# Second block's attention moved into slots 0 and 1, two tiles to a power, in a fused attention, feed-forward and soft-MoE kernel

## The chip, the cores and the metric

The kernel runs on one core of a Trainium2 chip. The metric is device time in microseconds (us), the median of several runs. The engines are TensorE (PE, with its weight loads PEld), VectorE (DVE), ScalarE (ACT), GpSimd (POOL) and SyncE (SP), which issues most of the DMAs.

## The reference

```python
def _attn_ref(q, k, v, g_norm):
    kv = np.einsum('bhsd,bhse->bhde', k, v)
    out = np.einsum('bhsd,bhde->bhse', q, kv)
    rms = np.sqrt(np.mean(out * out, axis=-1, keepdims=True) + 1e-06)
    return (out / rms * g_norm).astype(np.float32)

def _moe_ref(x, w_in, w_out):          # x: 4608 x 512, w_in: 512 x 2048, w_out: 2048 x 512
    h = x @ w_in
    g = h * np.cos(h)
    return (g @ w_out).astype(np.float32)
...
# then a soft mixture: 32 slots, softmax over tokens, 8 experts, softmax over slots
```

Attention is linear: for each head a 64x64 matrix `kv`, then `q @ kv`, divided by its root mean square over the 64 columns of the head. Its output, 4608 tokens by 512, feeds the feed-forward layer, and that feeds the mixture.

## The kernel before

The 4608 tokens are cut into ten blocks, eight of 512 tokens (blocks 0 to 7) and two of 256. A block has tiles of 128 tokens. For a block, each of 16 **slots** f (feature tiles of 128 of the 2048 hidden columns) does one `main(j, f)`: 12 products of 128x512 in fp32r, since each operand is split in a high and a low part and three of the four part products are taken, over four slices of the 512 input columns. `h` comes out in one of three PSUM banks (pool `ps_m`). Then `fr_tt` (ACT, whole turns), `round_off` (DVE, rest), `cos_b` (ACT, sine table), `cos_c` (DVE, `h` times the cosine, named gT or q) follow, and `cos_c` frees the bank.

A tile of attention goes through four steps. `att_out` does the products with `kv` on PE, a square on ACT, a sum by head on DVE (L213), a scale (L214) and, on POOL, the power -1/2 of 8 sums for each token (L216, result `ri`). `att_xs` multiplies by `ri` on DVE (L223). `att_xT` transposes on PE (L241) and scales into the high part on ACT (L245); `att_lo` takes the low part on DVE (L254). The small tiles `ss` (the sums) and `ri` come from a pool whose `bufs` says how many live at once: a tile that takes a buffer again waits for all readers of the one before.

The sixteen weight tiles of `w_in` are made in six steps `A R P L H S`: A scales on ACT (L301), R, P, L work on bits on DVE (L306, L311, L316), H takes the high part on ACT (L322), S the low part on POOL (L327). All of them go through two staging buffers `st_m`. Small letters are the same steps of `w_out`.

Order is written out by hand. `PLAN["start"]` lists the work before slot 0: the attention of block 0 (`ao`, `xs`, `xT`, `lo`), weight tiles 0 and 1, and `warm.n`, n products of 128x128 that only fill PE. `one` lists the steps of slots 0 to 3, where only block 0 has mains; `two` those of slots 4 on, where block 0 and block 1 run in turn with a lag of four slots, so block 1's `x` must be ready at slot 4 (`m0` is block 0's main of the slot, `m1` block 1's, `s` the extra work of the slot, `p` what comes after `r`, `c` the last step). `PLAN["A"]` gives the slots in which `att_out` and the steps behind it run for blocks 1 and 2, `PLAN["ao"]`, `xs`, `xT`, `lo` for later blocks, one block ahead of use. From block 2 on a slot has one main.

```python
        ss = sm_p.tile([128, H], F32, tag="ss", name="ss", bufs=4)
        nc.vector.tensor_reduce(out=ss, in_=sq, axis=AX.X, op=ALU.add)
...
        nc.gpsimd.tensor_tensor(out=ri[:, :, 0], in0=ss, in1=mhalf, op=ALU.pow)
```

Of the kernel before, what the change touches and what calls it, by code (L numbers as in the profile page):

```python
# [37 lines left out]
    ),  # L38
    one='m0 e0 A R f0 P a l0 r0 p0 L r s0 b0 H p c0 S l',
    two='s0 m0 A R m1 a f0 e1 P L l0 f1 r0 r1 s1 l1 p0 r b0 H c0 e0 b1 p c1 l S p1',  # L40
    wm=(3, 5),
# [31 lines left out]
def tile_linear_attention__ffn_cos__soft_moe(  # L73
# [309 lines left out]
    def main(j, f, ps=None):  # L383
        if ps is None:
            ps = ps_m.tile([128, 512], F32, tag="h", name="h")
        w, x = w_t[f], xt_t[j]
        assert all((j, t) in x_done for t in range(TT[j])) and ("S", f, 0) in done
        n = 0
        for kk in range(KD):
            for a, b in ((0, 0), (0, 1), (1, 0)):  # L390
                nc.tensor.matmul(out=ps, lhsT=w[:, a, kk, :], rhs=x[b][:, kk, :],  # L391
                                 start=(n == 0), stop=(n == 3 * KD - 1))
                n += 1
        h_t[j, f] = ps
# [583 lines left out]
    for b in range(1, B):  # L978
# [4 lines left out]
        for pr in range(4):  # L983
            at2(n, sl[pr], kv_pair, b, pr)

    for j in range(1, NB):
        n = min(j - 1, SMALL - 1)
# [101 lines left out]
    def token(t, f):  # L1089
        k, *arg = t.split(".")  # L1090
        if k.upper() in steps:
            out = int(k.islower())
            ws = [int(arg[0])] if arg else [w for w in range(NF) if PLAN["co"][w] == f] if out else [f + PLAN["LI"]]
            for w in ws:
                if w < NF and (arg or out or w >= PLAN["PI"]):
                    ck(k.upper(), w, out)
                    steps[k.upper()](w, out)
        elif arg:
            a = int(arg[0])
            dict(kv=lambda: kv_pair(0, a), ao=lambda: att_out(0, a), xs=lambda: att_xs(0, a),  # L1100
                 xT=lambda: att_xT(0, a), lo=lambda: att_lo(0, a), warm=lambda: warm(a),
                 win=lambda: load_win(a), wout=lambda: load_wout(a), lkv=lambda: load_kv(a // 4, a % 4),
                 rem=lambda: load_rem(a) if a == 0 else load_kz(0, 1),
                 q=lambda: [load_q(a, t) for t in range(3 if a else TT[0])])[k]()
        else:
# [6 lines left out]
    with tc.manual_schedule():  # L1112
# [132 lines left out]
```

## Time and profile before

| what | value |
|---|---|
| median of 3 runs | 675.74 us (674.06, 675.74, 676.40) |
| the profiled execution's own time | 674.39 us |
| its span, first to last instruction | 672.6 us |
| PE busy | 646.0 us, 96% of the span |
| DVE, ACT, POOL busy | 496.1, 328.1, 208.3 us |
| granted TensorE clock, mean | 0.991 of full speed |

The span is what the trace shows, and lies 1.8 us under the execution's own time. A busy time is a sum over the span. A row of the timeline gives start, length, engine, line, operation and count, and in brackets how long the engine had been idle and what ended that. PE records of f32 products are passes: a product of 128x128 in f32 has two, a transpose and an fp32r product one.

### The profile page before, as it was taken

The page shows a single profiled execution, that of the slowest core. Times are in us where ns is not written, and L with a number is a line of the kernel's source. Part 1 is how long each engine was busy: PE and PEld are TensorE (multiplying, and loading weights), DVE is VectorE, ACT ScalarE, POOL GpSimd, SP SyncE. Part 2 cuts the span into 40 slices and gives each one's busy share as a digit, 9 for nine tenths or more (in the row PEclk, how much of TensorE's full clock was granted, in tenths as well). Part 3 has the DMA queues.
Part 4 walks back from the last instruction along what each step waited for, and adds up shares of the span by engine and source line. Part 5 has one row for each costly group of instructions (what it writes and reads, how often), then busy time and mean ns, then how long its engine had stood idle before and what let it go on. Part 6 is the DMA issues. An engine that isn't in the chain of part 4 may idle for free.

```text
span 672.6 us, 12593 instructions
## 1 busy us (share of the span) xinstructions
PE 646.0 (96%) x4639; PEld 474.7 (71%) x4639; DVE 496.1 (74%) x909; ACT 328.1 (49%) x589; POOL 208.3 (31%) x291
## 2 busy tenths in 40 slices
PE   6989999999999999999999999999999999999992
PEld 6767777776667776767677677767677778984451
DVE  3799989966677778877887788787877765546143
ACT  3576767645244454445444554544463453552042
POOL 2451111320363333530643253334526322200000
PEclk9899999999999999999999999999999999999997
DMA  9955564111385636783677287576645369899998
GB/s 328 346 192 188 189 228 149 60 35 63 84 200 141 173 79 187 209 234 118 170 212 209 66 207 208 158 212 148 162 122 118 70 166 315 295 413 408 406 416 353
DMA packets 70589, 135.13 MB, mean 201 GB/s; under 512 B 10752, under 2 KB 39040, under 8 KB 69504
## 3 DMA queue, kind: packets, MB, share of 16 engines
q1 hardware_dynamic: 63360, 119.63, 54.3%
q0 software_dynamic: 7168, 14.69, 9.5%
q8 instruction: 37, 0.61, 0.4%
q14 instruction: 24, 0.20, 0.1%
HBM read 91.29 MB, written 13.63 MB: 156 GB/s over the span
## 4 chain that ended last, share of the span: by engine, by line
PE 76%; DVE 8%; ACT 5%; DMA 5%; SPq 2%; issue 2%; POOL 1%; DVEq 0%; ACTq 0%
PE h L391 46%; PE ab L624 5%; PE ops L202 4%; PE l L525 3%; PE xTps L241 2%; PE eh L780 2%; PE eo L817 2%; DMA g<-tr 2%; PE kvps L183 2%; PE tr L494 2%; DVE gT L453 2%; PE l L534 2%; DVE tmp L410 2%; ACT tmp L414 1%; SPq L513 1%
## 5 line engine op out<-in xcount | busy, mean ns | idle before, releaser
L391 PE MATMUL h<-xt,w 128*128 128x512 f32 (+1 forms) x1920 | 420.8, 374 | 3.6 <-DVE gT L453 1.5
L391 PEld LDWEIGHTS h<-xt,w 128*128 128x128 f32 x1920 | 329.4, 189 | 86.4 <-issue 12.7
L414 ACT ACTIVATE tmp<-tmp,hpi 128x512 f32<-128x512 f32 (+1 forms) x145 | 104.2, 720 | 174.2 <-DVE tmp L410 174.1
L513 POOL DMA_DIRECT2D g<-tr x224 | 123.4, 554 | 102.5 <-DVE tr L472 48.8
L453 DVE TENSOR_TENSOR gT<-tmp,h 128x512 f32<-128x512 f32 x130 | 89.1, 686 | 70.5 <-ACT tmp L414 70.5
L216 POOL TENSOR_TENSOR ri<-ss,mhalf 128x8 f32<-128x8 f32 x36 | 59.5, 1655 | 203.7 <-DVE ss L214 203.5
L410 DVE SCALAR_TENSOR_TENSOR tmp<-h,tmp 128x512 f32<-128x512 f32 (+1 forms) x145 | 97.1, 673 | 18.1 <-ACT tmp L407 17.2
L407 ACT ACTIVATE tmp<-h 128x512 int32<-128x512 f32 (+1 forms) x145 | 85.1, 587 | 46.7 <-PE h L391 46.4
L472 DVE STREAM_TRANSPOSE tr<-gT 128x512 f32<-128x512 f32 x103 | 73.2, 711 | 5.9 <-DMA g<-tr 1.6
L327 POOL TENSOR_TENSOR w<-st_m,w 128x512 fp32r<-128x512 f32 x16 | 21.4, 1335 | 63.8 <-ACT w L322 63.8
L202 PE MATMUL ops<-kvA,q 128*128 128x128 f32 (+1 forms) x320 | 38.6, 278 | 0.1
L245 ACT ACTIVATE xt<-xTps,gn 128x512 fp32r<-128x512 f32 x36 | 24.5, 685 | 25.7 <-PE xTps L241 25.7
L202 PEld LDWEIGHTS ops<-kvA,q 128*128 128x128 f32 (+1 forms) x320 | 34.6, 180 | 3.0 <-issue 2.0
L624 PE MATMUL ab<-g,d 128*32 128x512 f32 x256 | 32.3, 593 | 0.0
L525 PE MATMUL l<-gT,wp 128*32 128x512 f32 (+1 forms) x248 | 30.9, 556 | 0.0
L254 DVE SCALAR_TENSOR_TENSOR xt<-xTps,gn,xt 128x512 fp32r<-128x512 f32 x36 | 26.1, 729 | 4.8 <-ACT xt L245 4.6
L211 ACT ACTIVATE sq<-ops 128x512 f32<-128x512 f32 x31 | 18.5, 596 | 21.7 <-PE ops L202 21.6
L213 DVE TENSOR_REDUCE ss<-sq 128x8 f32<-128x512 f32 x31 | 21.0, 676 | 7.5 <-ACT sq L211 7.2
L183 PEld LDWEIGHTS kvps<-kv 128*64 128x64 f32 x448 | 15.4, 137 | 12.5 <-issue 7.6
L624 PEld LDWEIGHTS ab<-g,d 128*32 128x32 f32 x256 | 9.5, 110 | 19.2 <-issue 16.6
L223 DVE TENSOR_TENSOR sq<-ops,ri 128x512 f32<-128x512 f32 x31 | 20.9, 675 | 1.2 <-POOL ri L216 1.2
L241 PE MATMUL xTps<-ident,sq 128*128 128x128 f32 x124 | 19.0, 276 | 1.8 <-DVE sq L223 1.8
(186 smaller groups left out, 605.3 us busy)
## 6 DMA issues: line engine op xcount, KB each, us to landing
kv<-in_kv SPq DMA_DIRECT2D x28, 512.0 KB, 5.7
g<-tr SPq DMA_DIRECT2D x224, 64.0 KB, 3.7
g<-tr POOLq DMA_DIRECT2D x224, 64.0 KB, 3.8
ew<-in_ew SPq DMA_DIRECT2D x23, 512.0 KB, 8.9
q<-in_qT SPq DMA_DIRECT2D x36, 256.0 KB, 6.0
out<-ot SPq DMA_DIRECT2D x11, 768.0 KB, 7.5
rw<-in_w_in SPq DMA_DIRECT2D x16, 512.0 KB, 4.2
nat<-in_w_out SPq DMA_DIRECT2D x16, 512.0 KB, 3.9
```

The lines of the kernel that those rows point to most:

```text
L202: nc.tensor.matmul(out=ps[p0:p0 + n, pr * 128:(pr + 1) * 128], lhsT=q_t[j, t][:, pr, p0:p0 + n], rhs=kvbd[b % 2][:, pr, :], start=True, st ...
L216: nc.gpsimd.tensor_tensor(out=ri[:, :, 0], in0=ss, in1=mhalf, op=ALU.pow)
L241: nc.tensor.transpose(ps[:, kk * 128:(kk + 1) * 128], xs[:, kk * 128:(kk + 1) * 128], ident)
L391: nc.tensor.matmul(out=ps, lhsT=w[:, a, kk, :], rhs=x[b][:, kk, :], start=(n == 0), stop=(n == 3 * KD - 1))
L407: nc.scalar.activation(out=t.bitcast(I32), in_=ps, func=AF.Copy, bias=0.25, scale=INV_2PI)
L410: nc.vector.scalar_tensor_tensor(out=t, in0=ps, scalar=INV_2PI, in1=t.bitcast(I32), op0=ALU.mult, op1=ALU.subtract)
L414: nc.scalar.activation(out=t, in_=t, func=AF.Sin, bias=hpi, scale=TWO_PI)
L453: nc.vector.tensor_tensor(out=g, in0=fr, in1=h_t.pop((j, f)), op=ALU.mult)
L472: nc.vector.transpose(out=tr_t[j, q][:, :, i, :], in_=gT_t[j, n * q + i].rearrange("p (b t) -> p b t", t=32))
L513: (nc.gpsimd if b % 2 else nc.sync).dma_start(out=dst[32 * b:32 * b + 32, :, x, a:a + n, :].rearrange("p t f i -> p t (f i)"), in_=src[32 ...
L525: nc.tensor.matmul(out=l_t[j][32 * o:32 * o + 32, :], lhsT=wp[:, f, :], rhs=gT_t.pop((j, f)), start=(c == 0), stop=(c == (2 if j == NB - 1 ...
L624: nc.tensor.matmul(out=ps[32 * c:32 * c + 32, :], lhsT=d[:, t, :], rhs=gs[c // 2][t][:, (c % 2) * 512:(c % 2) * 512 + 512], start=(t == 0) ...
```

## The change

In the start list, `keep.7` adds seven filling products in a bank of `ps_m` between block 0's `att_out` and its first transpose; the last two `warm` lose one product; `xs.3` goes ahead of the first `lo`; scale A of weight tile 2 moves ahead of `lo.3`. The first main takes its products with the high part of `x` first. Slot 0 and slot 1 get lists of their own: `turn_on` in slot 0 does H and S of weight tile 2 and A, R, P of tile 3, so that S of tile 3 stands at slot 1's head. From slot 2 on, A is that of the tile one further on and stands before H. Block 1's `att_out` run in slots 0, 0, 1, 1, and its tiles share `ss2`, `ri2` in pairs, with one power of 128x16 for two tiles. The single `ss` and `ri`, which blocks 0 and 2 to 9 use, have two buffers, where there were four. The fourth `q` tile of block 1 is loaded with the other three, in a staging buffer. For blocks 3 on, the second `att_out` runs in slot 4, where it was in slot 5.

```diff
-        "kv.3 lkv.7 rem.1 q.1 win.3 wout.0 wout.1 wout.2 ao.0 ao.1 ao.2 ao.3 A.0 xs.0 xT.0 warm.4 xs.1 R.0 P.0 xT.1 "
-        "xs.2 L.0 H.0 S.0 xT.2 warm.3 lo.0 xs.3 lo.1 xT.3 lo.2 A.1 lo.3 R.1 P.1 L.1 H.1 S.1 "
+        "kv.3 lkv.7 rem.1 q.1 win.3 wout.0 wout.1 wout.2 ao.0 ao.1 ao.2 ao.3 keep.7 A.0 xs.0 xT.0 warm.4 xs.1 R.0 P.0 xT.1 "
+        "xs.2 L.0 H.0 S.0 xT.2 warm.2 xs.3 lo.0 lo.1 xT.3 lo.2 A.1 A.2 lo.3 R.1 P.1 L.1 H.1 S.1 "
...
-    one='m0 e0 A R f0 P a l0 r0 p0 L r s0 b0 H p c0 S l',
-    two='s0 m0 A R m1 a f0 e1 P L l0 f1 r0 r1 s1 l1 p0 r b0 H c0 e0 b1 p c1 l S p1',
+    one0='m0 e0 R f0 P l0 r0 p0 L s0 b0 c0',
+    one1='m0 e0 L f0 H S a l0 r0 p0 r s0 b0 A p c0 l',
+    one='m0 e0 R f0 P a l0 r0 p0 L r s0 b0 A H p c0 S l',
+    two='s0 m0 R m1 a f0 e1 P L l0 f1 r0 r1 s1 l1 p0 r b0 A H c0 e0 b1 p c1 l S p1',
...
-    A=(((0, 0, 1, 2), (1, 1, 1, 1), (2, 2, 3, 3), (0, 0, 0, 0)),
+    A=(((0, 0, 1, 1), (1, 1, 1, 1), (2, 2, 3, 3), (0, 0, 0, 0)),
...
-    ao=(2, 5, 8, 11),
+    ao=(2, 4, 8, 11),
...
-        ss = sm_p.tile([128, H], F32, tag="ss", name="ss", bufs=4)
+        pair = j == 1
+        if pair and t % 2:
+            s2, r2 = two.pop()
+        elif pair:
+            s2, r2 = (sm_p.tile([128, 2 * H], F32, tag=x, name=x, bufs=1) for x in ("ss2", "ri2"))
+            two.append((s2, r2))
+        if pair:
+            ss, ri = s2[:, t % 2 * H:t % 2 * H + H], r2[:, t % 2 * H:t % 2 * H + H].rearrange("p (h o) -> p h o", o=1)
+        else:
+            ss = sm_p.tile([128, H], F32, tag="ss", name="ss", bufs=2)
+            ri = sm_p.tile([128, H, 1], F32, tag="ri", name="ri", bufs=2)
...
-        ri = sm_p.tile([128, H, 1], F32, tag="ri", name="ri", bufs=4)
-        nc.gpsimd.tensor_tensor(out=ri[:, :, 0], in0=ss, in1=mhalf, op=ALU.pow)
+        if pair and t % 2:
+            nc.gpsimd.tensor_tensor(out=r2, in0=s2, in1=mhalf[:, 0:1].to_broadcast([128, 2 * H]), op=ALU.pow)
+        elif not pair:
+            nc.gpsimd.tensor_tensor(out=ri[:, :, 0], in0=ss, in1=mhalf, op=ALU.pow)
...
+        order = [(kk, a, b) for kk in range(KD) for a, b in ((0, 0), (0, 1), (1, 0))]
+        if (j, f) == (0, 0):
+            order.sort(key=lambda o: o[2])
...
+    def turn_on():
+        for k, w in (("H", 2), ("S", 2), ("A", 3), ("R", 3), ("P", 3)):
+            ck(k, w, 0)
+            steps[k](w, 0)
+
+    at(0, 0, turn_on)
```

Three places show how the instructions stand. The first is DVE in the start list, block 0's four tiles; `ss_...` are the sums, `st_x` the squares and later the scaled tiles, `ri_...` the powers, and the brackets name the semaphores of the engines that an instruction waits for. Before:

```order
L213 TENSOR_REDUCE ss_260<-st_x_126 128x8 [waits Activation_49]
L213 TENSOR_REDUCE ss_271<-st_x_126 128x8 [waits Activation_49]
...
L213 TENSOR_REDUCE ss_282<-st_x_126 128x8 [waits Activation_49]
L214 TENSOR_SCALAR ss_282<-ss_282 128x8 [waits DVE_49]
L223 TENSOR_TENSOR st_x_126<-ops_243,ri_252 128x512 [waits PE_49,Pool_49]
```

With the change:

```order
L228 TENSOR_REDUCE ss_261<-st_x_126 128x8 [waits Activation_49]
L228 TENSOR_REDUCE ss_272<-st_x_126 128x8 [waits Activation_49,Pool_49]
...
L228 TENSOR_REDUCE ss_283<-st_x_126 128x8 [waits Activation_49,Pool_49]
L229 TENSOR_SCALAR ss_283<-ss_283 128x8 [waits DVE_49]
L240 TENSOR_TENSOR st_x_126<-ops_244,ri_251 128x512 [waits PE_49]
```

The third and fourth sums now also wait for POOL, and the first multiplication by `ri` still stands behind the fourth sum.

The second is POOL from the start into slot 3: powers `ri`, and S of the weight tiles (`w`). Before:

```order
L216 TENSOR_TENSOR ri<-ss,mhalf 128x8 [waits DVE_49] x4
L327 TENSOR_TENSOR w<-st_m,w 128x512 [waits DMAHW4_49,Activation_49]
L327 TENSOR_TENSOR w<-st_m,w 128x512 [waits DMAHW5_49,Activation_49]
L216 TENSOR_TENSOR ri<-ss,mhalf 128x8 [waits DVE_49,Pool_49] x2
L327 TENSOR_TENSOR w<-st_m,w 128x512 [waits DMAHW0_49,Activation_49]
L216 TENSOR_TENSOR ri<-ss,mhalf 128x8 [waits DVE_49,Pool_49]
```

With the change:

```order
L233 TENSOR_TENSOR ri<-ss,mhalf 128x8 [waits DVE_49] x2
L233 TENSOR_TENSOR ri<-ss,mhalf 128x8 [waits DVE_49,Pool_49] x2
L344 TENSOR_TENSOR w<-st_m,w 128x512 [waits DMAHW4_49,Activation_49]
L344 TENSOR_TENSOR w<-st_m,w 128x512 [waits DMAHW5_49,Activation_49]
L344 TENSOR_TENSOR w<-st_m,w 128x512 [waits DMAHW0_49,Activation_49]
L231 TENSOR_TENSOR ri_443<-ss_442,mhalf 128x16 [waits DVE_49]
L344 TENSOR_TENSOR w<-st_m,w 128x512 [waits DMAHW0_49,Activation_49]
L231 TENSOR_TENSOR ri_495<-ss_494,mhalf 128x16 [waits DVE_49,Pool_49]
```

S of tile 2 now stands ahead of block 1's powers, and four powers of 128x8 became two of 128x16.

The third is PE in block 3, slots 3 to 6: `ldT` is a transpose of the block before's logits, `ops` the products of `att_out`, `xTps` those of `att_xT`. Before:

```order
L391 MATMUL h<-xt,w 128x512 x24
L594 MATMUL ldT<-ident,ld 128x64 x4
L391 MATMUL h<-xt,w 128x512 x12
L241 MATMUL xTps<-ident,sq 128x128 x4
L202 MATMUL ops<-kvA,q 128x128 x4
L391 MATMUL h<-xt,w 128x512 x12
```

With the change:

```order
L409 MATMUL h<-xt,w 128x512 x24
L611 MATMUL ldT<-ident,ld 128x64 x4
L207 MATMUL ops<-kvA,q 128x128 x4
L409 MATMUL h<-xt,w 128x512 x12
L258 MATMUL xTps<-ident,sq 128x128 x4
L409 MATMUL h<-xt,w 128x512 x12
```

The second `att_out` now stands between `ldT` and the main of slot 5. Blocks 4 to 7 are the same.

## Rows read from the trace of the kernel before

**Rows 1.** The page, busy us, share of the span and instructions of each engine

```profile
PE 646.0 (96%) x4639; PEld 474.7 (71%) x4639; DVE 496.1 (74%) x909; ACT 328.1 (49%) x589; POOL 208.3 (31%) x291
```

**Rows 2.** Waits of PE: who for whom, us in total, times, longest

```profile
PE xTps L241 <- DVE st_x L223: 2.3, 1, 2.3
...
PE xTps L241 <- DVE sq L223: 1.8, 1, 1.8
PE h L391 <- DVE gT L453: 1.5, 6, 0.3
...
PE h L391 <- POOL w L327: 1.0, 1, 1.0
```

**Rows 3.** Windows: stretch, length, busy us (instructions) of PE, PEld, DVE, ACT, POOL, PEclk, DMA

```profile
30.00:48.00 18.00, 15.22 (x101) 12.80 (x97) 16.43 (x32) 12.98 (x24) 10.23 (x7) 1.00 0.64 217
48.00:65.00 17.00, 16.74 (x98) 13.52 (x96) 16.53 (x29) 12.61 (x24) 4.07 (x3) 1.00 0.45 161
65.00:90.00 25.00, 25.00 (x174) 19.43 (x173) 24.67 (x41) 17.48 (x36) 3.93 (x3) 1.00 0.60 211
```

**Rows 4.** Timeline of the start, block 0's attention to the first main

```profile
13.75 6.57 POOL L216 TENSOR_TENSOR ri<-ss,mhalf 128x8 f32<-128x8 f32 x4 [11.54 <-DVE ss L214]
...
14.56 0.69 DVE L213 TENSOR_REDUCE ss<-st_x 128x8 f32<-128x512 f32 x1
...
16.17 0.17 DVE L214 TENSOR_SCALAR ss<-ss 128x8 f32<-128x8 f32 x1
16.26 1.50 DVE L223 TENSOR_TENSOR st_x<-ops,ri 128x512 f32<-128x512 f32 x2
...
20.60 0.68 DVE L223 TENSOR_TENSOR st_x<-ops,ri 128x512 f32<-128x512 f32 x1
...
22.23 0.60 PE L241 MATMUL xTps<-ident,st_x 128*128 128x128 f32 x4
22.87 0.69 ACT L245 ACTIVATE xt<-xTps,gn 128x512 fp32r<-128x512 f32 x1 [0.72 <-PE xTps L241]
...
23.61 0.50 PE L391 MATMUL h<-xt,w 128*128 128x512 f32 x1 [0.78 <-ACT xt L245]
...
24.40 2.83 PE L391 MATMUL h<-xt,w 128*128 128x512 f32 x11 [0.28 <-DVE xt L254]
```

**Rows 5.** Windows of 1 us in the start, columns as in the third group

```profile
19.00:20.00 1.00, 0.94 (x5) 0.78 (x5) 1.00 (x3) 0.00 (x0) 1.00 (x1) 0.50 1.01 406
```

**Rows 6.** Timeline of slots 0 to 5: idle DVE, PE's waits, H on ACT

```profile
27.45 1.05 DVE L306 TENSOR_SCALAR st_m<-st_m 128x512 int32<-128x512 int32 x1 [1.32 <-ACT st_m L301]
...
31.34 0.69 DVE L213 TENSOR_REDUCE ss<-sq 128x8 f32<-128x512 f32 x1 [0.92 <-ACT sq L211]
...
32.90 0.62 ACT L322 ACTIVATE w<-st_m 128x512 fp32r<-128x512 f32 x1
...
36.90 2.56 PE L391 MATMUL h<-xt,w 128*128 128x512 f32 x10 [1.03 <-POOL w L327]
...
47.16 0.63 PE L241 MATMUL xTps<-ident,sq 128*128 128x128 f32 x4 [1.75 <-DVE sq L223]
...
56.24 1.20 DVE L311 SCALAR_TENSOR_TENSOR st<-st 128x512 int32<-128x512 int32 x1
```

**Rows 7.** Groups on POOL by form: busy us, mean ns of one

```profile
L216 POOL TENSOR_TENSOR ri<-ss,mhalf 128x8 f32<-128x8 f32 x36 | 59.5, 1655 | 203.7 <-DVE ss L214 203.5
L327 POOL TENSOR_TENSOR w<-st_m,w 128x512 fp32r<-128x512 f32 x16 | 21.4, 1335 | 63.8 <-ACT w L322 63.8
...
L1229 POOL MEMSET const-float32-1.0<- 128x1 f32 x1 | 0.1, 98 | 0.0
```

**Rows 8.** Timeline of block 4, slots 4 to 6

```profile
310.05 0.69 DVE L453 TENSOR_TENSOR gT<-tmp,h 128x512 f32<-128x512 f32 x1 [1.32 <-ACT tmp L414]
310.08 0.46 PE L594 MATMUL ldT<-ident,ld 64*128 64x64 f32 x4
...
310.79 3.02 PE L391 MATMUL h<-xt,w 128*128 128x512 f32 x12 [0.25 <-DVE gT L453]
...
314.09 1.06 PE L202 MATMUL ops<-kvA,q 128*128 128x128 f32 x8
```

More of the change, by code (lines that the diff above doesn't have):

```diff
@@ L151, in load_q @@
             q_t[j, t] = first["q"][:, t]
+        elif (j, t) == (1, 3):
+            q_t[j, t] = first["wo"][3].rearrange("p (r c) -> p r c", r=4)
         else:
@@ L195, in tile_linear_attention__ffn_cos__soft_moe @@
     kv_done, x_done, g_done = set(), set(), set()
+    two = []
     def att_out(j, t):
@@ L204, in att_out @@
                                  start=True, stop=True)
-        if (j, t) == (1, 2):
-            sq = first["wo"][2].rearrange("p (h d) -> p h d", d=D)
+        if j == 1 and t > 1:
+            sq = first["wo"][4 - t].rearrange("p (h d) -> p h d", d=D)
         elif j:
@@ L387, in main @@
         assert all((j, t) in x_done for t in range(TT[j])) and ("S", f, 0) in done
[L388 to L393, printed above, removed]
+        order = [(kk, a, b) for kk in range(KD) for a, b in ((0, 0), (0, 1), (1, 0))]
+        if (j, f) == (0, 0):
+            order.sort(key=lambda o: o[2])
+        for n, (kk, a, b) in enumerate(order):
+            nc.tensor.matmul(out=ps, lhsT=w[:, a, kk, :], rhs=x[b][:, kk, :],
+                             start=(n == 0), stop=(n == 3 * KD - 1))
         h_t[j, f] = ps
@@ L744, in c_lo, with warm @@
         nc.vector.tensor_tensor(out=lo, in0=ps, in1=hi.bitcast(F32), op=ALU.subtract)
-    def warm(n):
-        ps = at_bank("warm")
+    def warm(n, ps=None):
+        if ps is None:
+            ps = at_bank("warm")
         for _ in range(n):
@@ L994, in tile_linear_attention__ffn_cos__soft_moe @@
             i = T0[j] + t + 3
-            if i < NT:
+            if 7 < i < NT:
                 jj = max(x for x in range(NB) if T0[x] <= i)
@@ L1092, in token @@
             out = int(k.islower())
-            ws = [int(arg[0])] if arg else [w for w in range(NF) if PLAN["co"][w] == f] if out else [f + PLAN["LI"]]
+            ws = [int(arg[0])] if arg else [w for w in range(NF) if PLAN["co"][w] == f] if out else [f + PLAN["LI"] + (k == "A")]
             for w in ws:
-                if w < NF and (arg or out or w >= PLAN["PI"]):
+                if w < NF:
                     ck(k.upper(), w, out)
@@ L1099, in token @@
             a = int(arg[0])
-            dict(kv=lambda: kv_pair(0, a), ao=lambda: att_out(0, a), xs=lambda: att_xs(0, a),
+            dict(kv=lambda: kv_pair(0, a), ao=lambda: att_out(0, a), xs=lambda: att_xs(0, a), keep=lambda: warm(a, ps_m.tile([128, 512], F32, tag="h", name="h")),
                  xT=lambda: att_xT(0, a), lo=lambda: att_lo(0, a), warm=lambda: warm(a),
@@ L1103, in token @@
                  rem=lambda: load_rem(a) if a == 0 else load_kz(0, 1),
-                 q=lambda: [load_q(a, t) for t in range(3 if a else TT[0])])[k]()
+                 q=lambda: [load_q(a, t) for t in range(4)])[k]()
         else:
@@ L1135, in tile_linear_attention__ffn_cos__soft_moe @@
         for f in range(NF):
-            for t in (PLAN["one"] if f < L else PLAN["two"]).split():
+            for t in PLAN[f"one{f}" if f < 2 else "one" if f < L else "two"].split():
                 token(t, f)
```

## The prediction

> **What bounds the kernel now.** I read the page first: PE is busy 646.0 of 672.6 us [rows 1], so only what PE idles can be won without less work, some 27 us. The waits of PE come next, since they say where that idleness lies and who ends it. Outside the first load and the tail they are few: 2.3 us before block 0's first transpose, which waits for the multiplication by `ri`; 1.8 once before a transpose of block 1; 1.0 once for a weight tile's low part on POOL; and six waits for gT of 0.3 at most [rows 2]. The windows then tell which engine paces the work behind those waits. From 30 to 48 us DVE is busy 16.43 of 18.00, from 48 to 65 it is busy 16.53 of 17.00 while PE is 16.74, and from 65 to 90 PE is full and DVE 24.67 of 25.00 [rows 3]. So from 30 to 90 us two engines are nearly full, and a lead that PE gets in slots 0 to 3 lasts only if DVE gets it too. That is the point on which the start's part of the sum turns. In blocks 3 to 7 the waits for gT are one in each block, 0.25 in block 4, in slot 5, because the cosine came late from ACT [rows 8].
>
> **The start list.** All times here are those of the trace. Block 0's four powers run one behind the other from 13.75, 6.57 us in all, 1.64 each, and the four sums ran ahead of them [rows 4]. With two buffers, the third sum must wait until the first power has read its buffer: 15.39, where it began at 14.56. The fourth waits for the second power: 17.04. Its scale begins 0.72 later (as 14.56 was followed by 15.28), and the first multiplication, which is queued behind it on DVE, at 17.9, where it was at 16.26. The third power needs the buffer of the first `ri`, so that multiplication must end first: 17.9 and 0.7 is 18.6. Third and fourth power end at 21.9, where they ended at 20.32. So the new wait stops the queue of DVE, and through it POOL's, PE's and ACT's.
>
> The fourth multiplication begins at 21.9, where it was 20.60; the list puts it ahead of the low part that it stood behind, so it is 1.3 late and not 1.6. It ends at 22.6. Two filling products (four passes at 1.06/8, which is 0.13 [rows 8], together 0.5) and the transpose follow, and ACT takes its step 0.64 after the transpose began (22.23 to 22.87), at 23.7, where it was 22.87. The first main begins 0.74 behind that, at 24.45, where it was 23.61: **0.83 late**. Its products with the low part come last now, so the hole between 23.61 and 24.40 goes: 12 products take 3.1 instead of 3.6, and it ends 0.3 late. DVE is 0.83 late with the low part, as ACT is.
>
> The seven filling products are fourteen passes at 0.13, 1.8 us, and lie in the hole of 2.3 before the first transpose. But that hole moves: PE now idles some 2 us behind them, until 18.6. The granted clock was 0.50 at 19 to 20 us, which is 1.2 GHz, after that idleness [rows 5]. I expect the same again. It costs nothing where PE waits for the powers anyway. If the first main still ran at 1.2 GHz, its 12 products would cost 12 x 0.24 more, 2.9, of which the hole of DVE in slot 0 (next part) takes 2.0: so 0 to 0.9, and I take 0, since the clock was full again before that main in the trace and PE's work ahead of it is of the same kind.
>
> **Slots 0 to 5.** PE loses both its waits there, 1.03 and 1.75 [rows 6]: S of tile 2 stands ahead of the powers, and block 1's last two tiles come a slot earlier. With 0.3 lost at the start, PE could reach slot 4 as much as 2.5 us early. DVE decides what is left of that. It starts 0.83 late. Its idleness of 1.32 before R of tile 2 goes, since A of that tile is earlier, and so does the 0.92 before block 1's first sum [rows 6]. But R of tile 3 now stands there and waits for A of tile 3, which on ACT stands behind the eight copies of `kv`, which end 0.3 late, and behind H of tile 2. The first sum could begin at 31.34 because a square of 0.6 had begun at 30.7, and ACT was free for it from 30.2. From 30.5, H takes 0.62 and A about as much, so R can begin at 31.75. DVE will have been free since 31.34 - 0.92 - 1.32 + 0.83, which is 29.9, or a little earlier: a new hole of 1.9 to 2.2. In all 0.83 - 2.24 + 2.0 is 0.6 late. Bit steps of DVE that fall on a POOL step are long (1.05 and, in 56.24's row, 1.20 [rows 6]); which ones do will change, worth 0.5 either way. Short holes in 30 to 65 (2.0 in all by rows 3, of which 0.92 is counted) may give back a few tenths. I take **0.5 late** at slot 5, bounds -0.3 and 1.2. PE's lead ends in waits for gT in slots 4 and 5.
>
> **The power of two tiles.** The trace has the power only at 128x8, 1.655 [rows 7]. At 128x16 it costs at least that, if the price is by instruction. At most it costs twice that less one start of an instruction, for which a memset of 128x1 at 0.098 stands: 3.21. I take 2.0, near the lower end: a subtraction costs 1.335 for 512 columns, 0.0026 a column, and with twenty such steps for a power (a guess, no row has it) eight more columns cost 0.4. Between the second scale and the multiplication that waits for the power stand three steps of DVE in the first pair (gT, L, rest; about 1.7 in all) and four in the second (2.2). So 2.0 costs 0.3 - 0 = **0.3**, 1.66 costs nothing, and 3.21 costs 1.5 + 1.0 = 2.5.
>
> Apart from these rows there is a rule: the Trainium skill's page "GPSIMD Engine Reference", section 3.1, has GpSimd spend a dispatch for each instruction and then cycles for each element, nothing else, so that a pair would save one dispatch alone. It has no price for a power; by it the sum would be that of the first rival. The subtraction's row fits it, and no row here shows a second width of the power.
>
> **Blocks 2 to 7.** In blocks 3 to 7, the second `att_out` fills the wait of slot 5. In block 4, gT ended at 310.74, `ldT` began at 310.08 and the main at 310.79. With eight passes between (1.06), the main starts behind gT and the wait is gone. The idle time was 0.25; the time lost was up to 0.4, since passes that follow each other overlap in the stream and `ldT`'s 0.46 holds its drain. Five times 0.35 is **-1.75**, bounds 0 and -2.1. The sum and scale that come earlier (0.69 and 0.17 [rows 4]) lie on a DVE that has holes there, 1.32 in that row alone. In block 2 they go ahead of the copy `d` for which the slot sums wait: 0 to 0.86, I take 0.2. A ahead of H in each slot delays H and the second cosine by 0.6 and frees ACT at the next slot's head; a weight tile has a slot of slack, so 0. The removed loads and the earlier `q` tile shift SP's queue by 256 KB in the start; tile 3, behind it, is needed over 10 us after its issue: 0.
>
> **Sum.** 0.5 + 0.3 + 0.2 - 1.75 = -0.75 against the profiled execution's own 674.39 (span 672.6 and 1.8 around it): 673.6. That execution lies 1.35 under the median of the runs, 675.74, so for a median I give **675.0**.
>
> **Rivals.** (1) The power is paid by column, 3.21. DVE stands 1.5 and 1.0 before the two pairs in place of 0.3: +2.2, so 1.45 over before, 677.2; with a first main at 1.2 GHz (+0.9) 678.1. This is the slower side, and it decides from a power of about 2.5, where the two waits (0.8 and 0.3) eat the rest of the gain. For it: the small price of starting an instruction [rows 7]. Against: eight columns would have to cost eighty times a subtraction's each. (2) DVE does catch up: its bit steps miss POOL's, and PE keeps 1.7 of its 2.5 at slot 4. Then -1.7 + 0.2 - 1.75 is -3.25, 672.5. For it: both of PE's large waits go. Against: 16.53 of 17.00 [rows 3]. (3) The wait in blocks 3 to 7 moves to the next main, as DVE has more to do before it: +1.0, 676.7. Against: the slot sums of slot 6 (16 products) give DVE time.
>
> **Chances.** Forecast 0.47, rivals 0.28, 0.13, 0.12. A measurement of this kernel tells 0.3%, 2.0 us, from no change: under 673.7 is faster, over 677.8 slower. Faster: most of rival 2 and a fifth of the forecast, 0.21. Slower: half of rival 1 and a little of rival 3, 0.17. Within: 0.62. The range runs from rival 2 to rival 1 with the half clock: 672.6 to 678.2.
>
> **What would show it.** Third and fourth sum of block 0 at about 15.4 and 17.0, the first multiplication at 17.9, the first main at 24.4; no wait for w in slot 2; DVE idle some 2 us before R of tile 3; two powers of 128x16 and their length; waits for gT in slots 4 and 5; no wait of the main of slot 5 in blocks 3 to 7. The forecast is wrong if the sums run through without POOL, if main (0,4) keeps its lead at 65 us, or if the power is over 2.5.

## The result and the profile after

The changed kernel takes **679.38 us** (median, 677.4 to 680.25) beside 674.12 for the kernel before: ratio 1.0068, 95% interval 1.0046 to 1.009, so 3 to 6 us slower. A second timing gave 679.18 and 1.0069 (1.0054 to 1.0084). The prediction said 675.0, between 672.6 and 678.2; the outcome lies above its range. The profiled execution (679.47, span 677.7) stands for the median; its own counterpart before has a span of 672.6.

The page's busy times answer to [rows 1]. PE has 12 filling passes more (fourteen of `keep.7`, two fewer of `warm`) and ran some of its start at the lower clock (below); the other engines do the work they did:

```profile
PE 649.0 (96%) x4651; PEld 475.3 (70%) x4651; DVE 496.4 (73%) x909; ACT 328.0 (48%) x589; POOL 208.8 (31%) x289
```

PE's waits after (who for whom, us in total, times, longest) beside [rows 2]. The wait for `w` is gone and that of 1.8 is broken up, but the one for `st_x` is as long as ever, gT's are fewer and three times as long, and a wait for the DMA of `g` is new:

```profile
PE xTps L258 <- DVE st_x L240: 2.4, 1, 2.4
PE h L409 <- DVE gT L470: 2.3, 3, 1.0
...
PE ab L641 <- DMA g<-tr: 1.5, 1, 1.5
...
PE tr L511 <- DVE A L240: 0.8, 1, 0.8
...
PE tr L511 <- DVE q L470: 0.7, 1, 0.7
PE xTps L258 <- DVE xt L271: 0.6, 1, 0.6
```

DVE's waits after, of which before had only one of 1.6 for `g` and one of 1.2 in its line of the multiplication by `ri` (L240 here):

```profile
DVE tr L489 <- DMA g<-tr: 2.2, 1, 2.2
...
DVE ss L228 <- POOL ri L233: 1.6, 2, 0.9
...
DVE sq L240 <- POOL ri L233: 1.2, 1, 1.2
DVE sq L240 <- POOL ri L231: 1.2, 1, 1.2
DVE tr L489 <- DMA nat<-in_w_out: 1.2, 1, 1.2
...
DVE A L240 <- POOL ri L231: 0.8, 1, 0.8
```

The windows of [rows 3], after (length, busy us and instructions of PE, PEld, DVE, ACT, POOL, PEclk, DMA): DVE is busy 13.81 of 18.00 where it was 16.43, and in the next stretch nearly full again, with PE at 15.24 where it was 16.74. What DVE lost by 48 us PE pays by 65:

```profile
30.00:48.00 18.00, 15.99 (x116) 13.03 (x112) 13.81 (x26) 12.11 (x24) 9.14 (x5) 1.00 0.63 220
48.00:65.00 17.00, 15.24 (x88) 11.87 (x89) 16.83 (x27) 11.50 (x22) 3.47 (x3) 1.00 0.23 77
```

The start after, to be held against [rows 4] (timeline: start, us, engine, line, operation). Third and fourth sum wait for powers; the third power waits for the first multiplication, and so do PE's first transposes, which then take 1.09 (the granted clock is 0.50 from 19 to 21 us):

```profile
15.43 0.69 DVE L228 TENSOR_REDUCE ss<-st_x 128x8 f32<-128x512 f32 x1 [0.90 <-POOL ri L233]
...
17.04 0.69 DVE L228 TENSOR_REDUCE ss<-st_x 128x8 f32<-128x512 f32 x1 [0.72 <-POOL ri L233]
...
17.84 1.28 DVE L240 TENSOR_TENSOR st_x<-ops,ri 128x512 f32<-128x512 f32 x2
...
18.68 1.09 PE L258 MATMUL xTps<-ident,st_x 128*128 128x128 f32 x4 [2.35 <-DVE st_x L240]
18.68 3.24 POOL L233 TENSOR_TENSOR ri<-ss,mhalf 128x8 f32<-128x8 f32 x2 [1.67 <-DVE st_x L240]
...
21.95 0.69 DVE L240 TENSOR_TENSOR st_x<-ops,ri 128x512 f32<-128x512 f32 x1 [0.31 <-POOL ri L233]
...
22.79 0.68 PE L767 MATMUL warm<-ident 128*128 128x128 f32 x4
...
23.52 0.66 PE L258 MATMUL xTps<-ident,st_x 128*128 128x128 f32 x4
```

Slots 0 to 3 after: the hole before R of tile 3, and the two powers of 128x16 with the multiplications that wait for them and the transposes that wait for the second of these:

```profile
32.17 1.05 DVE L323 TENSOR_SCALAR st_m<-st_m 128x512 int32<-128x512 int32 x1 [1.94 <-ACT st_m L318]
...
35.63 2.89 POOL L231 TENSOR_TENSOR ri<-ss,mhalf 128x16 f32<-128x16 f32 x1 [2.69 <-DVE ss L229]
...
38.55 1.29 DVE L240 TENSOR_TENSOR sq<-ops,ri 128x512 f32<-128x512 f32 x2 [1.21 <-POOL ri L231]
...
41.58 2.90 POOL L231 TENSOR_TENSOR ri<-ss,mhalf 128x16 f32<-128x16 f32 x1 [1.80 <-DMA q<-in_qT]
...
44.52 0.69 DVE L240 TENSOR_TENSOR A<-ops,ri 128x512 f32<-128x512 f32 x1 [0.82 <-POOL ri L231]
...
45.26 0.66 PE L511 MATMUL tr<-ident,q 128*128 128x128 f32 x4 [0.83 <-DVE A L240]
```

Two groups on POOL by form (busy us, mean ns) give what [rows 7] did not have, the second width:

```profile
L233 POOL TENSOR_TENSOR ri<-ss,mhalf 128x8 f32<-128x8 f32 x32 | 53.0, 1656 | 180.6 <-DVE ss L229 169.2 <-DMA g<-tr 9.7 <-DVE st_x L240 1.7
...
L231 POOL TENSOR_TENSOR ri<-ss,mhalf 128x16 f32<-128x16 f32 x2 | 5.8, 2896 | 4.5 <-DVE ss L229 2.7 <-DMA q<-in_qT 1.8
```

Later places, PE and DVE. In block 4 the main of slot 5 starts without a wait, as forecast [rows 8]. The **slot sums** (PE's products `ab`, which add up the mixture's 32 slots) read `g`, a copy of gT that DMAs regroup from DVE's transposes `tr`; in block 2's slots they wait for these DMAs. A transpose of block 6 on DVE waits for `g` too, and 11 us behind it a main waits for gT:

```profile
200.24 0.59 PE L641 MATMUL ab<-g,d 128*32 128x512 f32 x1 [1.47 <-DMA g<-tr]
...
316.95 3.01 PE L409 MATMUL h<-xt,w 128*128 128x512 f32 x12
...
464.43 0.71 DVE L489 STREAM_TRANSPOSE tr<-gT 128x512 f32<-128x512 f32 x1 [2.25 <-DMA g<-tr]
...
475.14 3.03 PE L409 MATMUL h<-xt,w 128*128 128x512 f32 x12 [0.37 <-DVE gT L470]
```

**The yardstick for what follows.** For each kernel the table has how much later (+) its mains start than the same mains of the kernel before, from PE's timeline of one execution of each: main 1 (slot 0; 23.61 before), 2 (31.51), 5 (slot 4; 47.98), 10 (64.41), 39 and 40 (190.18 and 198.41, on both sides of a slot sum), 103 (439.14) and the last (600.22). Medians and ratios are of the timed runs.

| kernel | median | ratio (95%) | 1 | 2 | 5 | 10 | 39 | 40 | 103 | last |
|---|---|---|---|---|---|---|---|---|---|---|
| changed | 679.38 | 1.0068 (1.0046-1.009) | 1.35 | 0.74 | 0.87 | 3.59 | 3.64 | 5.36 | 4.60 | 5.25 |
| e1_bufs4 | 676.02 | 1.0031 (1.0014-1.0048) | -0.63 | 0.35 | 0.45 | 3.18 | 3.24 | 4.25 | 2.95 | 2.33 |
| e2_single | 673.87 | 1.0002 (0.9983-1.002) | -0.41 | -1.01 | -2.64 | 0.07 | 0.14 | 0.85 | -0.43 | -0.74 |
| e3_lateq | 677.20 | 1.0046 (1.0029-1.0064) | 1.47 | 0.86 | 0.98 | 3.70 | 3.76 | 4.69 | 3.42 | 3.21 |
| e4_ao | 673.23 | 0.9989 (0.9977-1.0001) | -0.77 | -0.80 | -0.80 | -0.82 | -0.77 | -0.46 | -1.73 | -1.89 |
| e5_again | 679.18 | 1.0069 (1.0054-1.0084) | 1.38 | 0.78 | 0.90 | 3.62 | 3.67 | 5.50 | 4.23 | 4.74 |
| e6_bufs2 | 676.43 | 1.0034 (1.0021-1.0046) | 2.31 | 2.27 | 2.26 | 2.27 | 2.29 | 2.05 | 1.98 | 1.46 |
| e7_single_n2 | 674.71 | 1.0016 (0.9999-1.0033) | -0.26 | -0.87 | -2.50 | 0.22 | 0.21 | 0.97 | -0.30 | -0.71 |
| e8_HA | 674.56 | 1.0001 (0.9986-1.0015) | -0.21 | -0.82 | -2.44 | -0.23 | -0.21 | -0.32 | -1.60 | -1.62 |
| e9_ao3 | 672.96 | 0.9978 (0.9963-0.9993) | -0.20 | -0.25 | -0.23 | -0.24 | -0.24 | 0.12 | -1.18 | -1.59 |
| e10_ao3_lateq | 673.45 | 0.9988 (0.9977-0.9999) | -0.71 | -0.67 | -0.65 | -0.63 | -0.64 | 0.22 | -1.06 | -0.82 |
| e11_keep | 673.98 | 0.9992 (0.9983-1.0002) | -0.95 | -1.56 | -1.56 | -1.56 | -1.56 | -1.05 | -1.03 | -1.13 |
| e12_both | 672.58 | 0.9976 (0.9959-0.9993) | -0.96 | -1.56 | -1.57 | -1.58 | -1.54 | -0.77 | -2.05 | -2.24 |
| e13_n2 | 677.53 | 1.0078 (1.005-1.0105) | 1.18 | 0.57 | 0.70 | 3.42 | 3.45 | 3.98 | 2.68 | 2.48 |

One caution on the first columns: e4, e9 and e10 share the start of the kernel before, and their first mains still stand 0.2 to 0.8 earlier. The granted clock is one reason: 0.50 at 19 to 21 us before, 1.00 there in e4. So a difference under 0.8 in these columns may be the execution's.

### The profile page after: what moved, and what is told of

It is laid out like the page before. It is cut to its first block, busy times and chain, and to the rows that moved or that the text cites. A ratio compares the mean times of both kernels' runs of the same rounds, so it can differ in the third digit from the quotient of the medians.

```text
span 677.7 us, 12604 instructions
## 1 busy us (share of the span) xinstructions
PE 649.0 (96%) x4651; PEld 475.3 (70%) x4651; DVE 496.4 (73%) x909; ACT 328.0 (48%) x589; POOL 208.8 (31%) x289
## 4 chain that ended last, share of the span: by engine, by line
PE 68%; DVE 16%; DMA 5%; ACT 5%; issue 2%; POOL 1%; SPq 0%; DVEq 0%; ACTq 0%; POOLq 0%
PE h L409 42%; PE ops L207 4%; PE ab L641 3%; DVE tmp L427 3%; PE l L542 3%; DVE gT L470 3%; ACT tmp L431 2%; DVE tr L489 2%; PE eh L798 2%; PE eo L835 2%; PE kvps L187 2%; PE tr L511 2%; PE l L551 2%; PE xTps L258 2%; DMA g<-tr 1%
## 5 line engine op out<-in xcount | busy, mean ns | idle before, releaser
L427 DVE SCALAR_TENSOR_TENSOR tmp<-h,tmp 128x512 f32<-128x512 f32 (+1 forms) x145 | 96.9, 672 | 18.0 <-ACT tmp L424 17.5
L233 POOL TENSOR_TENSOR ri<-ss,mhalf 128x8 f32<-128x8 f32 x32 | 53.0, 1656 | 180.6 <-DVE ss L229 169.2
L424 ACT ACTIVATE tmp<-h 128x512 int32<-128x512 f32 (+1 forms) x145 | 85.1, 587 | 44.7 <-PE h L409 44.4
L187 PEld LDWEIGHTS kvps<-kv 128*64 128x64 f32 x448 | 15.4, 137 | 12.6 <-issue 7.7
L240 DVE TENSOR_TENSOR sq<-ops,ri 128x512 f32<-128x512 f32 x30 | 20.2, 676 | 2.4 <-POOL ri L233 1.2
L187 PE MATMUL kvps<-kv 128*64 128x64 f32 x448 | 18.3, 226 | 2.1 <-DMA kv<-in_kv 2.1
```

Source lines behind the costliest of these rows:

```text
L187: nc.tensor.matmul(out=ps[h], lhsT=t[:, 0, r, h], rhs=t[:, 1, r, h], start=(r == 0), stop=False)
L424: nc.scalar.activation(out=t.bitcast(I32), in_=ps, func=AF.Copy, bias=0.25, scale=INV_2PI)
L427: nc.vector.scalar_tensor_tensor(out=t, in0=ps, scalar=INV_2PI, in1=t.bitcast(I32), op0=ALU.mult, op1=ALU.subtract)
```

## The experiments

### Two buffers: e1_bufs4 and e6_bufs2

The change with four buffers again, and the kernel before with two:

```diff
-ss = sm_p.tile([128, H], F32, tag="ss", name="ss", bufs=2)
-ri = sm_p.tile([128, H, 1], F32, tag="ri", name="ri", bufs=2)
+ss = sm_p.tile([128, H], F32, tag="ss", name="ss", bufs=4)
+ri = sm_p.tile([128, H, 1], F32, tag="ri", name="ri", bufs=4)
```

> The changed kernel with four buffers again for the single tiles' ss and ri; nothing else. In the changed kernel's trace DVE waited 0.90 and 0.72 us for POOL before the third and fourth sum of block 0, and the first main came 1.35 late (24.96 after 23.61). Theory S (the start's wait is carried to slot 5, since DVE is nearly full from there on): the sums stand at 14.5 and 15.4 again, the first main at 23.6 or earlier, DVE reaches slot 5 some 1.3 to 1.6 earlier, and the run takes about 678.0 where the change takes 679.4. Theory P (the powers of two tiles and the step A behind the copies of kv set the pace of slots 0 to 4 by themselves): the hole before R of tile 3 (1.94) grows by what the start saves, and the time stays within 0.5 of the changed kernel's.

> The kernel before, with two buffers in place of four for ss and ri and nothing else of the change. Theory S: third and fourth sum at 15.4 and 17.0, the first main 0.8 to 1.35 late, and DVE carries 1.0 to 1.6 of it past slot 5: 675.1 to 675.7. Rival: DVE's holes of 1.32 and 0.92 in slots 0 and 1 of the kernel before take it up: 674.1 to 674.4.

Measured: the change drops from 679.2 to 676.02, and the kernel before rises from 674.25 to 676.43, more than the 675.1 to 675.7 of theory S. In e6 the start's loss of 2.3 passes unchanged from main 1 to main 39: DVE's holes take up nothing, as theory S has it. Not all of the 2.3 is the sums' wait: PE idles 3.91 without a filler, and its transposes then run at the clock's lower level, 1.2 GHz (0.50, last but two columns):

```profile
18.74 1.09 PE L241 MATMUL xTps<-ident,st_x 128*128 128x128 f32 x4 [3.91 <-DVE st_x L223]
```

```profile
20.00:21.00 1.00, 1.00 (x7) 1.00 (x6) 0.83 (x2) 0.55 (x1) 1.00 (x2) 0.50 1.04 418
```

The e1 trace looks like theory P (0.41 gained at main 10), but its first main ran at 1.2 GHz (granted clock 0.61, 0.50, 0.50 in the three us from 23), and its mains went from -0.63 to +0.35 by that. DVE waited 1.7 for ACT's first step behind that main (`DVE tmp L427 <- ACT tmp L424` in slots 0 to 5), in e2 0.2. Against e2, the same start at full clock (-1.01 at main 2), the half clock cost e1 1.36. If this is carried to main 10, as e6 and e11 carry what they lose and win in the start, two buffers cost 0.41 + 1.36 = **1.8** there. The medians, with the waits for `g` in them (below), say 3.2.

### The powers of two tiles: e2_single

```diff
-pair = j == 1
+pair = False
```

> As the run before it (four buffers), and block 1 takes one power per tile, as block 0 does; its output steps stay in slots 0, 0, 1, 1. In the changed kernel DVE waited 1.21 and 0.82 for the two powers of 128x16, 2.90 each, and PE 0.83, 0.60 and 0.69 behind the second. Theory P: with powers of 1.65 the first ri of each pair is there 2.1 earlier (the first sum's power runs beside the second sum), both holes of DVE go, and the time is about 2.0 under the kernel with four buffers. Rival: four powers keep POOL 0.8 us longer than two pairs, the low parts w of tiles 2 to 4 stand behind them, and DVE's holes go to other steps: within 0.5 of the kernel with four buffers.

Measured: 673.87, 2.15 under e1; theory P. The first of two powers now serves the first multiplication, and DVE's holes of 1.21 and 0.82 shrink to 0.34 and none. Timeline of POOL, then DVE:

```profile
33.15 3.34 POOL L233 TENSOR_TENSOR ri<-ss,mhalf 128x8 f32<-128x8 f32 x2 [1.95 <-DVE ss L229]
```

```profile
36.52 0.69 DVE L240 TENSOR_TENSOR sq<-ops,ri 128x512 f32<-128x512 f32 x1 [0.34 <-POOL ri L233]
```

At main 10 e1 and e2 differ by 3.11; 1.36 of it was there at main 2. So the pairs cost **1.75**, and DVE's three holes make 1.69 of it (1.21 and 0.82 less 0.34). And e2 shows what DVE's pace does: PE reaches slot 4 2.64 early and is level with the kernel before at main 10, after waits for gT of 0.95 before mains 8 and 10.

### H and A: e7_single_n2 and e8_HA

e7 is e2 with block 3's second att_out back in slot 5 (in block 2's slots); e8 is e7 with H and A swapped from slot 2 on:

```diff
+elif n == 2:
+    ao = (2, 5, 8, 11)
```

```diff
-one='m0 e0 R f0 P a l0 r0 p0 L r s0 b0 A H p c0 S l',
-two='s0 m0 R m1 a f0 e1 P L l0 f1 r0 r1 s1 l1 p0 r b0 A H c0 e0 b1 p c1 l S p1',
+one='m0 e0 R f0 P a l0 r0 p0 L r s0 b0 H A p c0 S l',
+two='s0 m0 R m1 a f0 e1 P L l0 f1 r0 r1 s1 l1 p0 r b0 H A c0 e0 b1 p c1 l S p1',
```

> The changed kernel with four buffers, one power per tile, and the second att_out of block 3 (the one that runs beside block 2's multiplications) in slot 5 again; for the later blocks it stays in slot 4. In the kernel before, that place had no wait of a main, and each run with slot 4 shows a wait of the slot sums for a g DMA at 195 to 200 us (0.3 to 1.5). Theory: this wait goes, and the time is 0.5 to 0.8 under the run with single powers (673.9), 673.2. Rival (the wait is due to something else that the change moved, A ahead of H for one): it stays, 673.9.

> As the run before it, and from slot 2 on H stands ahead of A again on ACT. In the run with single powers DVE is as late at the tenth gT as in the kernel before (72.12 and 72.15 us), though it idles 0.32 less, because three bit steps beside POOL's low parts w take 1.58, 1.79 and 1.69, where they took 1.19, 1.20 and 1.16. If H's place sets where POOL's low part falls, the three steps are back near 1.2, the mains from slot 5 on come 1.2 earlier, and the time is some 1.2 under the run before it, 672.0. Rival: POOL's low part moves 0.6 and meets other steps of DVE: no change within 0.5; or A, now 0.6 later, makes R wait: slower by up to 0.6 a slot for two or three slots.

Measured: e7 still loses 0.76 between mains 39 and 40, as e2 loses 0.71, so the rival holds: the wait has another cause. In e8 the colliding bit step falls from 1.78 to 1.41 and POOL's low part from 1.70 to 1.29. e7 (DVE, POOL), then e8 (POOL, DVE):

```profile
56.46 1.78 DVE L328 SCALAR_TENSOR_TENSOR A<-st,A 128x512 int32<-128x512 int32 x1
```

```profile
56.00 1.70 POOL L344 TENSOR_TENSOR w<-st_m,w 128x512 fp32r<-128x512 f32 x1 [6.05 <-DVE gT L470]
```

```profile
55.37 1.29 POOL L344 TENSOR_TENSOR w<-st_m,w 128x512 fp32r<-128x512 f32 x1 [5.50 <-ACT w L339]
```

```profile
55.79 1.41 DVE L328 SCALAR_TENSOR_TENSOR st<-st 128x512 int32<-128x512 int32 x1
```

That is worth 0.45 at main 10 (0.22 to -0.23), not 1.2: the mechanism holds, its size was a third of what I expected. The medians (674.71, 674.56) do not tell it.

### The second output a slot earlier: e4_ao, e9_ao3

The kernel before with this part alone; e9 leaves block 3's in slot 5:

```diff
-ao=(2, 5, 8, 11),
+ao=(2, 4, 8, 11),
```

> The kernel before, with the second att_out of blocks 3 to 7 in slot 4 in place of 5 and nothing else of the change. By the prediction's step alone: 1.75 earlier, 672.4. Theory Q: the five waits go (1.55 in the trace), but the q load that moves along costs the slot sums, the logits and a main 1.8, 0.5 and 1.0 again: 675.8, slower than before by 1.7. If the waits for g have to do with the start's delay, not with the load: 672.5.

> The kernel before with the second att_out of the later blocks in slot 4, but that of block 3, which runs beside block 2's multiplications, left in slot 5, where no main waited. Theory W (the five waits of 0.31 are won, and only block 3's move costs something): 1.55 under the kernel before, some 672.6, with no wait of the slot sums for g near 195 us. Rival: as with all six moved, 673.2, since the wait of 0.35 near 480 us, behind DVE's transposes that wait for g, stays.

Measured: in each block the main of slot 5 is 0.3 earlier for good: between mains 40 and 103 four of the five steps give -1.30 in e9, -1.27 in e4, where the change has -0.76 (one step of +0.50, at 307, goes against it). e9 takes 672.96, 1.3 under the kernel before (674.26): theory W. Its second half, no wait of the slot sums, fails: e9 loses 0.36 between mains 39 and 40 with nothing moved there. e4 takes 673.23, 0.8 under the kernel before (674.06), which its interval does not quite tell from none; theory Q's 675.8 did not come.

### The q load: e3_lateq, e10_ao3_lateq

Moving att_out moves the load of the q tile behind it, 256 KB on SP's queue, ahead of four `g` DMAs. The change, and e9, with that load where it was:

```diff
-ld_at(n, ao[t] + 1 + (n > 1), load_q, jj, i - T0[jj])
+ld_at(n, ao[t] + 1 + (n > 1) + (ao[t] == 4), load_q, jj, i - T0[jj])
```

> The changed kernel, with the load of the q tile that follows block 3 to 7's second att_out kept in the slot where it stood before the change (the load only; att_out itself stays in slot 4). Theory Q (that load, 256 KB, now stands ahead of the regrouping DMAs g on SP's queue, and what reads g comes later): the wait of the slot sums at 198.8 us (1.47) and of DVE's transposes at 276.5 (1.19) go, with them the main's 1.8, 0.5 and 1.0 us at 200, 307 and 475; the five waits of 0.31 that the change won stay won. About 676.3, where the change takes 679.4. Rival G (it is the power of 1.66 that moved ahead of POOL's own share of the g DMAs, or the DMA engines' load alone): the waits stay, 679.4 within 0.5.

> As the run before it, with the load of the q tile that follows the second att_out kept a slot later, where it stood in the kernel before. In the changed kernel the later load took 2.0 us off the median. Theory Q (the load ahead of the g DMAs costs by itself): 0.3 to 0.5 less than the run before it, 672.2. Theory V (the waits for g differ by where the whole run stands, and the gain of 2.0 was of that kind): no difference, within 0.4.

Measured: e3 takes 677.20, 2.0 under the change, but keeps 0.93 between mains 39 and 40, and e10 with 673.45 gains nothing over e9 (0.86 there). e1 and e2, with the load as the change has it, lose 1.01 and 0.71 there and nothing at 307 and 475. So the load isn't the cause, or not alone.

### The waits for g: e5_again, e13_n2, e14_look, e15_look

> The changed kernel once more, unedited. The runs with four buffers and with the later q load both lost the waits of 0.5 and 1.0 us at 307 and 475 us, though only one of them touched what the trace names there; so either the waits for DMA differ between executions of one kernel (theory V: this run's trace shows other sizes, the wait of the slot sums near 200 us between 0.3 and 1.8, and no or other waits at 307 and 475, and the median may come out near 678), or they belong to the changed kernel (theory Q: the same three waits again, 679.4).

> The changed kernel with block 3's second att_out alone back in slot 5, so that its power on POOL and the q load on SP stand behind the g DMAs again that block 2's slot sums read. Theory B (the two ahead of these g make the wait of 1.47 and 1.58 that both traces of the changed kernel show): it falls to the 0 to 0.9 that the runs with neither ahead show, and the time by about 1.0, to 678.2. Theory V (the wait is whatever the DMA queues leave at that moment): no change, 679.2 within 0.5. The waits near 307 and 475 us are not touched.

e13 is the change with the `elif` of e7 alone. The other three are the change, unedited.

> The changed kernel, unedited, one look. Its eleven timed executions lie in two groups, four from 677.4 to 678.4 and seven from 679.2 to 680.3; both profiled ones were of the upper group, with waits for g DMAs of 1.5 to 1.6 (slot sums near 200 us) and 2.1 to 2.2 (DVE's transpose near 464 us). If these waits vary between executions and make the difference, a look of the lower group shows smaller ones (by 1 to 2 us in sum), and one of the upper group the same again.

> The changed kernel, unedited, a second look; as for the first: time and the two waits go together, or the waits are the same in both groups and the difference lies elsewhere.

Measured: four executions of the same program lose 1.72, 1.83, 1.48 and 0.10 between mains 39 and 40, and 0.98, 0.87, 0.29 and 0.24 between mains 103 and 114 (near 475). PE's row of the slot sum in e14; e15 has no such wait:

```profile
199.88 0.59 PE L641 MATMUL ab<-g,d 128*32 128x512 f32 x1 [1.23 <-DMA g<-tr]
```

So theory V: they vary from one execution to the next. e14 took 677.63, 1.5 to 1.8 less than the first two, whose losses are large in both places. e15 still took 678.32, since it lost 1.5 behind its last main; part of that is a wait of PE for the load of the expert weights:

```profile
PE eo L835 <- DMA ew<-in_ew: 0.3, 1, 0.3
```

That stretch behind the last main differs in other runs too, against the kernel before from -0.85 (e8) to +3.12 (e4, whose PE waits 1.3 for these loads), so one execution's time says little about an edit. e13 took 677.53, from 676.6 to 683.0. Its trace loses 0.53 between mains 39 and 40, as theory B has it, but e15 loses 0.10 with both ahead, so e13 does not decide. Over all traces, kernels with power and q load both ahead of these `g` (the changed one, e1, e2, e4) lose 0.10 to 1.83 there, those with neither (before, e6 to e13) -0.24 to 0.86. Whether the two make the wait larger on average stays open.

### What the change has that pays: e11_keep, e12_both

The kernel before with the filler and the sorted first main; e12 adds the edit of e9:

```diff
-... ao.2 ao.3 A.0 xs.0 ...
+... ao.2 ao.3 keep.7 A.0 xs.0 ...
...
+order = [(kk, a, b) for kk in range(KD) for a, b in ((0, 0), (0, 1), (1, 0))]
+if (j, f) == (0, 0):
+    order.sort(key=lambda o: o[2])
```

> The kernel before with the seven filling products behind block 0's att_out and the first main's products sorted by x, nothing else. The filler takes 1.73 us of the 2.31 that PE idles before the first transpose, and the granted clock should stay at 1.00 until the first main, where the trace of before shows 0.50 from 19 to 22 us; the first main then starts at 22.8 to 23.2 in place of 23.61 and ends without the hole of 0.28. If DVE alone paces slots 0 to 5, nothing of it is left at slot 9: 674.1. If the start is carried: 0.5 to 0.8 less, 673.4.

> The kernel before with the filling products, the sorted first main, and the later blocks' second att_out in slot 4 (block 3's in slot 5): the parts of the change that seem to be worth something, without the pairs, the two buffers and A ahead of H. The sum of its parts: 1.55 and 0 to 0.7 under the kernel before, 671.9 to 672.6. Rival: the waits for g near 460 us take one half of it back, 673.3.

Measured: in e11 PE's wait falls from 2.31 to 0.75, the granted clock stays 1.00, the first main starts at 22.66 without its hole, and the 1.56 won by main 2 are still there at main 39. PE of e11:

```profile
16.86 0.63 PE L241 MATMUL xTps<-ident,st_x 128*128 128x128 f32 x4 [0.75 <-DVE st_x L223]
...
22.66 2.56 PE L392 MATMUL h<-xt,w 128*128 128x512 f32 x10 [0.78 <-ACT xt L245]
```

Up to 0.8 of the 1.56 is the half clock of the one execution it is held against, and the trace is that of the fastest of its eleven runs. The median gains only 0.3 (673.98 after 674.26; 0.9992, 0.9983 to 1.0002), nearer to the expectation without a carry. So the trace shows the start carried to main 39, and the median does not tell the gain from none. e12 takes **672.58**, ratio 0.9976 (0.9959 to 0.9993): faster than both kernels, by 1.7 and 6.8.

## Why the prediction was wrong

**The bill at main 10**, where the change stands 3.59 late, from differences of the table, one execution each: filler and sorted main -1.56 (e11); the other order of the start list, of block 1's outputs and of A, +1.63 (e2 less e11); the pairs +1.75; two buffers +1.77. Behind it: waits for DMAs and their followers +1.77 (the slot sums), +0.50 (307, behind DVE's 1.2 that the page puts down to `nat`) and +0.98 (475) in this execution, five slots -0.3 each.

**Start list: events right, price wrong.** The sums at 15.43 and 17.04, the first multiplication at 17.84 and the fourth at 21.95 are the forecast's 15.4, 17.0, 17.9 and 21.9. The first main came at 24.96, not 24.45, at full clock too (24.99 in e5): the four filling passes began 0.15 behind the multiplication, where I had no gap, and took 0.73 from start to the transpose, not 0.5. The failing step is the next one: I took the filler to be worth 0, since the hole only moves. By the trace of e11 filler and sorted products are worth 0.8 to 1.6 when the sums aren't held up (by its median 0.3), so the buffers' wait spoils a gain that the same change brings. And a first main at 1.2 GHz, put at 0 to 0.9, cost 1.36 in e1; in the change it ran at full clock.

**Slots 0 to 5: the step that failed most.** "In all 0.83 - 2.24 + 2.0 is 0.6 late", taken as 0.5. That DVE decides was right: e2's lead of 2.64 in slot 4 is gone by main 10. The hole before R came as forecast (1.94). But I let the end of DVE's old holes (2.24) pay for the start's delay, as if the rest of the new order were free. It isn't: e2 less e11 is +1.63. Of this 0.55 stands at main 2 already (-1.01 and -1.56), by the order of the start list. The collisions of DVE's bit steps with POOL's low part, 1.59 and 1.78 where before had 1.2, make 0.45 by e8, within the 0.5 that I had left open. The other 0.6 was not taken apart. And a delay in the start isn't absorbed: e6 and e11 carry theirs, +2.3 and -1.56, to main 39 to the last tenth. Without the pairs this step and the start come to 3.59 - 1.75 = 1.84 late, where I said 0.5.

**The power: rival 1's price.** I took 2.0 of a range of 1.655 to 3.21; it takes 2.896, over the 2.5 at which that rival decides. The forecast's own formula then gives 2.9 - 1.7 and 2.9 - 2.2, 1.2 and 0.7; DVE waited 1.21 and 0.82, and it cost 1.75 where I had 0.3. The guess of twenty elementwise steps at a subtraction's price per column had no row; of the two bounds the upper was near. A line through the two rows gives (2.896 - 1.656)/8 = 0.155 a column and 0.42 for the start; there is no third width, and the wide power also spreads its exponent from one column, which no run separates. The Trainium skill's page "GPSIMD Engine Reference", section 3.1, counts a dispatch for each instruction and cycles for each element. The two rows agree with that.

**Blocks 2 to 7.** -1.75 was forecast for blocks 3 to 7, and five times 0.3, about -1.55, came, in e9 as well. Block 2 got +0.2 with an upper end of 0.86; it cost 1.72 in this trace, 0.10 to 1.83 in four executions. I looked at the copy `d` there, but not at what else the slot sums read: `g`, for whose DMAs PE waits 1.5 in this trace and not at all in e15. I also left out that the q load moves with att_out. By e10 that costs nothing in the kernel before; in the change, where e3 without it took 2.0 less, it stays open.

**The sum.** By terms: pairs 1.45 over the forecast, start and slots 1.34, waits for DMAs 3.05 in this execution, five slots 0.2: 6.0, of which the tail gave 0.2 back; between the forecast's -0.75 and the measured span's +5.1 lie 5.85. The forecast of 675.0 stood on 675.74 for the kernel before; on the 674.12 of the result it would be 673.4, so the miss is 6.0 and not 4.4. By the medians, four buffers and single powers take the whole loss away: 679.38, 676.02 (e1), 673.87 (e2). Rival 1 was right in mechanism and alone gave 677.2; rival 2 didn't come, though e12 reaches its 672.5; rival 3 didn't come, the gain in blocks 3 to 7 stays.

## What to carry to other kernels

Where two engines are nearly full, a delay at the head isn't absorbed: cost each new wait on the engine that sets the pace and carry it to the end, and don't pay for it with that engine's old holes. A buffer count is a wait: list, for each tile of a rotation, who must have read it first. An instruction merged to save starts pays only if its start is the larger part; here, by the line through two widths, 0.42 of 1.66 was, and waiting for the second tile cost more. A change of several parts should be taken apart: those that e12 keeps paid 1.7 us, and the rest cost 6.8.

## What the runs showed of the hardware

A power on POOL took 1.656 at 128x8 and 2.896 at 128x16, 1.24 more for eight more columns.

DVE's two-input bit steps and POOL's subtraction take turns, by their rows. In all traces a bit step that begins while the subtraction runs (but for one within 0.005 of its begin) ends 0.54 to 0.56 behind the subtraction's end: in e7 56.46 + 1.78 is 58.24, behind 56.00 + 1.70, in e8 55.79 + 1.41 is 57.20, behind 55.37 + 1.29. So a step of 0.68 takes as long as the subtraction still has to go and 0.55 more, and the place of POOL's step sets the price. The other way round, a subtraction that begins beside a bit step takes longer than 1.28: in the change the step at 59.23 ends at 59.91, and the subtraction from 59.37 takes 1.70, to 1.16 behind that. The Trainium skill's page "GPSIMD Engine Reference", section 2, has GpSimd's SBUF read port shared with VectorE. These rows agree with it; no run tests the port itself.

The granted clock of one start differs between executions. With the start of the kernel before, in which PE idles 2.3, it fell to 0.50 (1.2 GHz) for some us in three profiled executions of four (before, e9, e10, not e4); with that of the change, which idles 2.4, in five of six (the change, e3, e13, e14, e15, not e5); with the filler and four buffers, where PE idles 0.75, in one of six (e1). And DMA landings differ between executions of one program by enough to move a slot sum by 1.7 us.
